# First output unit's loads, products and low parts inside the last MLP block, and rows of y in the order of need

## Chip, cores and metric

One core of one Trainium2 chip. The metric is the device time of one launch in microseconds, as the median of three runs; less is better. The kernel before takes 872.04 us (869.55 to 872.58).

## What is computed

One sequence of 2048 tokens of width 640, all in 32-bit floats:

```python
xn = layernorm(x)                               # no weights, eps 1e-5
q, k, v = split(xn @ wqkv)                      # 32 heads of 20
p = softmax(mask(q @ k.T * 20 ** -0.5))         # causal, window of 256 keys
s = heads_joined(p @ v) @ wo
h = relu(xn @ w1 + b1) ** 2                     # 640 -> 1536
g = silu(h @ w2 + b2)                           # 1536 -> 640
out = x + s * g
```

## The kernel before

Every product of the projections and of the MLP is made of three TensorE products: each operand is held as a rounded high part and the rest, its low part, and high times high, high times low and low times high are added up in PSUM.

A first phase normalizes and turns x, makes v, and makes q and k of the first heads. Then a loop of 256 steps (and a few more until its pipeline is empty) goes through 16 pairs of heads with 16 steps each: scores, row maxima, exponentials (`p32`) and, every fourth step, the product with v (`values`, written as `ops`). Its results go to DRAM as `o_d[g]`, one tensor for each quarter g of the tokens; row 20 of each head holds the sums of the exponentials.

Between these steps a generator, `filler`, hands out the other TensorE work one product at a time: the rest of q and k, then the MLP. The MLP's 1536 hidden columns are cut in two halves `hf`, the tokens in four blocks `b`; the eight blocks (hf, b) run one after the other, and the last one is (1, 1), tokens of tiles 4 to 7 (a tile is 128 tokens). A block makes its hidden part (`hps`), then eight groups of second products (`yps`): four tiles times two halves `nh` of the 640 columns. A group is evacuated by VectorE (line 969), which adds what the first half of the hidden columns gave (`yin`). `y` of the last block's four tiles stays in SBUF; `y` of the other twelve is stored to DRAM and read back later by `fetch_y`.

After the last block comes the output stage, `out_filler`. It has eight units u; unit u covers the two tiles `4*(u//2) + u%2` and that plus 2, so unit 0 is tiles 0 and 2, unit 1 is tiles 1 and 3. For a unit

- `load(u)` reads `o` with four transfers into `ob` and the inverse sums with one transfer, a broadcast over four rows of partitions, into `sums` (lines 1069 to 1080). The inverse sums of quarter g come from `invert`: a load of the sums, a reciprocal on VectorE, a store to `rec_d[g]`.
- `turn_out(u, 0)` multiplies `ob` by `sums` on VectorE in two cuts and rounds each to the high part `oT` on ScalarE (lines 1094, 1095). `turn_out(u, 1)` makes the low part on VectorE (1098) and, in the output stage, calls `silu(u)`: two activations on ScalarE over two tiles of y (1108).
- four groups (two tiles, two halves) of 15 products with `wo` follow on TensorE (`wops`, line 599). Each is evacuated by a product with y on VectorE (1157), then GpSimd adds x (1162) and the tile is stored.

`yps` and `wops` share three PSUM banks, so a group's first product waits for the evacuation of the group three before it. `wo` itself comes in five pieces (`raw`, three buffers), each rounded on ScalarE (773) and subtracted on VectorE (774); the fifth is `wo4h`, `wo4l`. All transfers go out from SP's queue, in the program's order; an SP instruction that must wait holds up all that follow. Every engine works its instructions in the order in which the Python code runs.

In `filler`, `late()` is called ahead of each of the last block's eight `yps` groups. Before the change it loads unit 0 as soon as quarter 0's inverse sums are on their way and returns, since all eight groups are handed out while the 256 steps still run; the lines behind its `return` never run. So `out_filler` begins with the remaining six reads of y, four reads of x, `silu(0)`, and then `turn_out(0, ...)`.

Of the kernel before, what the change touches and what calls it, by code (L numbers as in the profile page):

```python
# [15 lines left out]
P = 128  # L16
# [41 lines left out]
def attn_mlp_kernel(ctx: ExitStack, tc, x, wqkv, wo, w1, b1, w2, b2, out):  # L58
# [500 lines left out]
    def post(dst, src):  # L559
        posts.append((dst, src))  # L560
# [266 lines left out]
    def filler():  # L827
# [48 lines left out]
        xb, its = [xT[p][NB - 1] for p in range(2)], []  # L876

        def late():
            load(0)
            if state[2] < 10 ** 6:  # L880
                return
            j = lates[0]
            lates[0] += 1
            start_pieces()
            for f in release(1, True):
                f()
                held[0] -= 1
            invert(j)
            for _ in range(2):
                fetch_y()  # L890
            if j >= 2:
                load(1)
            if j == 3 or j == 5:
                load_res()
            if j >= 4:
                turn_out(0, 0)
            if j >= 5:
                turn_out(0, 1)

        for n, (hf, b) in enumerate(blocks):  # L900
            if n % NB == 0:
# [53 lines left out]
            for tt in range(4):  # L955
                t = b * 4 + tt
                place = [None]
                jobs = []

                def start(nh, hf=hf, t=t, place=place, idx=4 * (n - NB) + tt, end=n == NB - 1 and tt == 3, n=n, tt=tt):  # L960
                    sl = slice(nh * HALF, (nh + 1) * HALF)
                    ps = Acc(HALF, "yps")

                    def evac():
                        vload[0] += 0.5
                        if not nh:
                            place[0] = room_of("p32", "ysb") if n == last else wgt.tile([P, D], F32, tag="wgqh", name="ysb")
                        ysb = place[0]
                        nc.vector.tensor_add(ysb[:, sl], ps.tile, (yins[t] if hf else b2t)[:, sl])  # L969
                        ps.free(1.2)  # L970
                        if nh:
                            if n == last:
                                ybt[t] = ysb
                            else:
                                post(y_d[hf][:, t, :], ysb)
                            if hf:
                                del yins[t]
                                load_yin(idx + 2)
                            if end:
                                shut.discard("21")  # L980
                    return [ps, open_job(evac), 0]

                def product(jb, nh, fc):
                    ps, job, _ = jb
                    while (tt // 2, fc // 2) not in made:
                        if state[2] < 10 ** 6:
                            yield None
                        elif tasks:
                            finish()
                        else:  # L990
                            drain(backlog, 1)
                    for hp, wp in ((0, 0), (0, 1), (1, 0)):
                        jb[2] += 1
# [29 lines left out]

    lates = [0]

    def invert(j=99):
        for g in range(NB):
            over = state[2] >= 10 ** 6
            if not over and state[2] < stored(g) + 3:
                return  # L1030
            if g not in recs:
                rows = o_d[g].rearrange("p (h r) n -> (p h) r n", h=2)
                recs[g] = at2.tile([P, P], F32, tag="rec", name="rec")
                for par in range(2):
                    nc.sync.dma_start(recs[g][64 * par:64 * (par + 1)], rows[:, 32 * par + DH].rearrange("h (j n) -> h j n", n=P))
            elif recs[g] is not None and (state[2] >= stored(g) + 5 if not over else j >= 2 + g % 2):
                nc.vector.reciprocal(recs[g], recs[g])
                nc.sync.dma_start(rec_d[g].rearrange("a h (j n) -> (a h j) n", n=P), recs[g])
                recs[g] = None
# [4 lines left out]
        return wgt.tile([P, D], F32, tag=tag, name=name)  # L1044

    ybt = {}
    y_early = [((8 + j) % NT, w, i, j % 3) for j, (i, w) in enumerate([(i, w) for i in range(2) for w in "qk" for _ in range(3)])]
    y_room = []

    def fetch_y():  # L1050
        if y_early:
            t, w, i, k = y_early.pop(0)
            if not k:
                y_room.append((at, at1)[i].tile([P, S], F32, tag=f"{w}s{i}", name=f"y{w}{i}"))
            slot = y_room[-1][:, k * D:(k + 1) * D]
            nc.sync.dma_start(slot, y_d[1][:, t, :])
            ybt[t] = slot
# [4 lines left out]
    def load_res():  # L1062
        k = len(xts)
        if k < NT:
            t = in_order[k]
            xts[t] = room_of("p32" if k % 3 else "wgkh", "xres")
            nc.sync.dma_start(xts[t], x[t * P:(t + 1) * P, :])

    def load(u):
        if u in ld or u >= 2 * NB or recs.get(u // 2, 0) is not None:  # L1070
            return
        if u % 2 == 0:
            obs[u // 2] = bigp.tile([P, KC * BT], F32, tag="big", name=f"ob_{u // 2}")
        ob = obs[u // 2][:, u % 2 * 2 * D:(u % 2 + 1) * 2 * D].rearrange("p (c n) -> p c n", c=KC)
        sums = at2.tile([P, 2, P], F32, tag="osb" if u % 2 else "sums", name="sums").rearrange("p a n -> p (a n)")
        rows = o_d[u // 2].rearrange("p (h r) n -> (p h) r n", h=2)[:, 32 * (u % 2):32 * (u % 2) + VW]
        for k in range(4):
            nc.sync.dma_start(ob[32 * k:32 * k + H], rows[:, k:DH:4])  # L1078
        nc.sync.dma_start(sums, rec_d[u // 2][u % 2].unsqueeze(0).to_broadcast([4, H, MT]))
        ld[u] = (ob, sums)  # L1080
# [38 lines left out]
        return wo_part  # L1119

    def out_filler(wo_part):
        while y_early:
            fetch_y()
        while len(xts) < 4:
            load_res()
        silu(0)
        for u in range(2 * NB):
# [9 lines left out]
            for t2 in range(2):  # L1137
# [3 lines left out]
                for nh in range(2):  # L1141
# [8 lines left out]
                            mms.append((oT[u][:, op, c, t2 * P:(t2 + 1) * P], wo_part(wp, c)[:, sl]))  # L1150
                    yield from mm_group(ps, mms, 0.133)
                    invert()
                    for v in range(u + 1, u + 4):
                        load(v)

                    def evac(ps=ps, sl=sl, nh=nh, res=res, xt=xts[t], t=t):
                        nc.vector.tensor_mul(res[:, sl], ps, ybt[t][:, sl])
# [26 lines left out]
    with tc.manual_schedule(engines={E_.PE, E_.Activation, E_.DVE, E_.Pool, E_.SP}):  # L1184
# [7 lines left out]
        for s in range(steps):  # L1192
# [74 lines left out]
```

## Time and profile before

| | |
|---|---|
| median of three runs | 872.04 us |
| the profiled execution: its own time | 872.63 us |
| its span, first to last instruction | 870.8 us |
| TensorE busy in the span | 852.4 us (98%) |
| VectorE, ScalarE, GpSimd busy | 456.1, 423.1, 323.5 us |
| mean granted TensorE clock | 0.990 |

The profiled execution is 1.8 us longer than its span. Times inside it are microseconds from the span's start. A row of the timeline has start, duration, engine, line, operation, output<-inputs, count, and in brackets the engine's idle time before it and what ended it. A row of waits has the total, the times and the longest. "PEclk" is the granted clock, 1.00 is full speed. In a row of the table by stretches of time come: the stretch, its length, then the busy time of TensorE, of its weight loads, of VectorE, ScalarE and GpSimd, the clock, the DMA share and GB/s. Names of tiles have no numbers in the profile.

### The profile page before, as it was taken

What the parts mean: (1) busy time and instruction counts of PE and PEld (TensorE: products, weight loads), DVE (VectorE), ACT (ScalarE), POOL (GpSimd) and SP (SyncE); (2) the same over time, 40 slices, a digit from 0 to 9 for tenths busy, and PEclk for the clock granted to TensorE, in tenths of its full rate; (3) what the DMA queues carried; (4) which work ended last, traced back from release to release, by engine and by line L of the source; (5) the groups of instructions that cost most, each with busy time, mean ns of one, the idle gap of its engine ahead of it and who ended that gap; (6) DMA issues with size and microseconds to landing.
All of it is one profiled execution on the core that took longest, in us unless ns stands there. A gap on an engine that the chain in (4) does not pass through costs nothing.

```text
span 870.8 us, 26507 instructions
## 1 busy us (share of the span) xinstructions
PE 852.4 (98%) x10640; PEld 796.1 (91%) x10640; DVE 456.1 (52%) x1348; ACT 423.1 (49%) x808; POOL 323.5 (37%) x652
## 2 busy tenths in 40 slices
PE   9999999999999999999999999999999999997998
PEld 8999999888888999999999989999999999886997
DVE  7652136656567555455454466554454454334664
ACT  5222114545557754745735755835735646622321
POOL 6010002333333543533534533634634534502443
PEclk9999999999999999999999999999999999997999
DMA  7997587787799463273374255474475364458982
GB/s 266 307 400 281 167 224 245 267 256 258 242 276 303 100 213 120 61 233 91 102 226 153 78 160 150 143 233 128 112 243 132 113 205 136 127 161 207 228 225 77
DMA packets 94371, 166.50 MB, mean 191 GB/s; under 512 B 10920, under 2 KB 43816, under 8 KB 93224
## 3 DMA queue, kind: packets, MB, share of 16 engines
q1 hardware_dynamic: 94248, 164.80, 62.0%
q8 instruction: 84, 1.38, 0.7%
q14 instruction: 39, 0.32, 0.1%
HBM read 93.66 MB, written 70.52 MB: 189 GB/s over the span
## 4 chain that ended last, share of the span: by engine, by line
PE 93%; DMA 2%; DVE 2%; ACT 1%; issue 1%; SPq 1%; DVEq 0%
PE yps L468 20%; PE hps L468 20%; PE qkps L468 14%; PE ops L546 10%; PE vps L228 8%; PE wops L599 7%; PE stps L518 5%; PE sps L478 4%; PE qkps L205 3%; DMA ob<-o 1%; PE tps L172 1%; DMA yk<-y 1%; SPq L1078 0%; DVE junk L486 0%; DMA xt<-in_A_x_dram 0%
## 5 line engine op out<-in xcount | busy, mean ns | idle before, releaser
L486 DVE CUSTOM_DVE_ANT_0 junk<-sps,mask 128x384 bf16<-128x384 f32 (+2 forms) x512 | 272.6, 532 | 249.0 <-PE hps L468 71.9
L524 ACT ACTIVATE p<-stps 128x768 f32<-128x768 f32 (+2 forms) x256 | 197.3, 771 | 263.5 <-PE stps L518 212.1
L468 PE MATMUL yps<-w,hh 64*128 64x320 f32 x1536 | 230.8, 311 | 3.6 <-DVE ysb L969 3.2
L525 POOL TENSOR_SCALAR_AFFINE_SELECT p<-p 128x256 f32<-128x256 f32 x256 | 104.3, 407 | 335.3 <-ACT p L524 320.8
L468 PE MATMUL hps<-xb,w 64*128 64x256 f32 x2520 | 220.6, 283 | 0.0
L468 PEld LDWEIGHTS hps<-xb,w 64*128 64x128 f32 x2520 | 208.8, 187 | 5.5 <-issue 5.4
L468 PEld LDWEIGHTS yps<-w,hh 64*128 64x128 f32 x1536 | 186.5, 186 | 8.3 <-DVE ysb L969 4.7
L468 PE MATMUL yps<-w,hl 64*128 64x320 f32 x768 | 178.6, 311 | 0.0
L478 PE MATMUL sps<-ks,qs 60*128 60x384 f32 (+2 forms) x512 | 142.1, 341 | 0.3
L518 PE MATMUL stps<-qs,ks 62*128 62x384 f32 (+2 forms) x512 | 134.9, 332 | 0.0
L468 PEld LDWEIGHTS yps<-w,hl 64*128 64x128 f32 x768 | 117.2, 186 | 2.4 <-issue 2.3
L468 PE MATMUL qkps<-xT,wgkh 64*128 64x512 f32 x320 | 100.4, 395 | 0.0
L468 PE MATMUL qkps<-xT,wgqh 64*128 64x512 f32 x320 | 98.8, 393 | 0.0
L546 PE MATMUL ops<-p,vp 128*21 128x128 f32 (+1 forms) x2112 | 92.8, 313 | 0.0
L527 POOL TENSOR_SCALAR_AFFINE_SELECT p<-p 128x256 f32<-128x256 f32 x224 | 91.5, 409 | 0.0
L478 PEld LDWEIGHTS sps<-ks,qs 60*128 60x128 f32 x512 | 87.2, 185 | 2.8 <-DVE mt L486 1.3
L518 PEld LDWEIGHTS stps<-qs,ks 62*128 62x128 f32 x512 | 88.0, 188 | 0.5
L546 PEld LDWEIGHTS ops<-p,vp 128*21 128x21 f32 x2112 | 65.2, 100 | 22.1 <-issue 8.9
L599 PE MATMUL wops<-wo,oT 128*128 128x320 f32 x384 | 66.7, 326 | 8.4 <-ACT oT L1095 3.8
L228 PE MATMUL vps<-wv,xT 128*128 128x320 f32 x480 | 71.5, 308 | 0.0
L599 PEld LDWEIGHTS wops<-wo,oT 128*128 128x128 f32 x384 | 62.1, 202 | 9.4 <-ACT oT L1095 8.0
L228 PEld LDWEIGHTS vps<-wv,xT 128*128 128x128 f32 x480 | 70.5, 188 | 0.1
(104 smaller groups left out, 1174.2 us busy)
## 6 DMA issues: line engine op xcount, KB each, us to landing
ks<-k_d SPq DMA_DIRECT2D x64, 240.0 KB
qs<-q_d SPq DMA_DIRECT2D x64, 240.0 KB
xb<-xs SPq DMA_DIRECT2D x60, 256.0 KB
xs<-xT SPq DMA_DIRECT2D x8, 1280.0 KB
k_d<-shm SPq DMA_DIRECT2D x19, 512.0 KB
q_d<-shm SPq DMA_DIRECT2D x19, 512.0 KB
y<-ysb SPq DMA_DIRECT2D x28, 320.0 KB
o<-osb SPq DMA_DIRECT2D x64, 128.0 KB
```

What stands on the lines that cost most here:

```text
L172: nc.tensor.transpose(ps[:, t * P:(t + 1) * P], xns[t][:, c * P:(c + 1) * P], ident)
L205: nc.tensor.matmul(ps, wt[:, c, :], xT[part][b][:, c * BT + t0:c * BT + t0 + n], start=m == 1, stop=m == 3 * KC)
L228: nc.tensor.matmul(ps, xT[xp][b][:, c * BT + t * P: c * BT + (t + 1) * P], wv[wp][:, c, nh * HALF:(nh + 1) * HALF], start=first and m == 0 ...
L468: return nc.tensor.matmul(out, a[r], b_[r], skip_group_check=True, **kw)
L478: nc.tensor.matmul(ss[hh][:, :nk], qs[i][o, q * P:(q + 1) * P], ks[i][o, k0 * P:k0 * P + nk], start=True, stop=True)
L486: nc.vector.tensor_tensor_reduce(out=junk[:, :nk], in0=ss[hh][:, :nk], in1=mask[:, 3 * P - nk:], scale=1.0, scalar=-3.0e38, op0=ALU.add, o ...
L518: nc.tensor.matmul(tps[:, hh, :n], ks[i][o, kb * P:(kb + 1) * P], qs[i][o, kb * P:kb * P + n], start=True, stop=True)
L524: nc.scalar.activation(p32[:, :, :n], tps[:, :, :n], AF.Exp, scale=SCALE)
L525: nc.gpsimd.affine_select(p32[:, :, 0:P], p32[:, :, 0:P], pattern=[[0, 2], [1, P]], compare_op=ALU.is_ge, fill=0.0, base=0, channel_multip ...
L527: nc.gpsimd.affine_select(p32[:, :, 2 * P:], p32[:, :, 2 * P:], pattern=[[0, 2], [-1, P]], compare_op=ALU.is_gt, fill=0.0, base=0, channel ...
L546: nc.tensor.matmul(ot[r0:r0 + VW, c0:c0 + len(part), :], vps[p][:, kb // 4, kb % 4, hh, :], pt[:, hh, :].rearrange("p (t n) -> p t n", n=P ...
L599: nc.tensor.matmul(ps, a, b_, start=j == 0, stop=j == n - 1)
```

## The change

`late()` now counts its eight calls, j = 0 to 7: `load(0)` from j = 3, `load(1)` from j = 4, `turn_out(0, 0)` at j = 5, `turn_out(0, 1)` and `load(2)` from j = 6. The twelve early rows of y come in another order, the first six being tiles 0, 2, 1, 3, 8, 10, all read within the steps; the other six follow one by one, after each group of the output stage. `out_filler` no longer starts with reads of y, and loads at most one unit after each group. The `sums` tiles get three tags of their own in place of sharing the `osb` buffers; the first tile of x takes a `p32` buffer in place of `wgkh`.

```diff
         def late():
-            load(0)
-            if state[2] < 10 ** 6:
-                return
             j = lates[0]
             lates[0] += 1
-            start_pieces()
-            for f in release(1, True):
-                f()
-                held[0] -= 1
-            invert(j)
-            for _ in range(2):
-                fetch_y()
-            if j >= 2:
+            if j >= 3:
+                load(0)
+            if j >= 4:
                 load(1)
-            if j == 3 or j == 5:
-                load_res()
-            if j >= 4:
+            if j >= 5:
                 turn_out(0, 0)
-            if j >= 5:
+            if j >= 6:
                 turn_out(0, 1)
+                load(2)
...
                                 post(y_d[hf][:, t, :], ysb)
+                                if hf:
+                                    stored_y.add(t)
...
-    y_early = [((8 + j) % NT, w, i, j % 3) for j, (i, w) in enumerate([(i, w) for i in range(2) for w in "qk" for _ in range(3)])]
-    y_room = []
+    y_early = [((0, 2, 1, 3, 8, 10, 9, 11, 12, 14, 13, 15)[j], w, i, j % 3) for j, (i, w) in enumerate([(i, w) for i in range(2) for w in "qk" for _ in range(3)])]
+    y_room, stored_y = [], set()
 
     def fetch_y():
-        if y_early:
+        if y_early and y_early[0][0] in stored_y and (y_early[0][2] == 0 or whole[0]):
...
-            xts[t] = room_of("p32" if k % 3 else "wgkh", "xres")
+            xts[t] = room_of("p32" if k % 3 or k == 0 else "wgkh", "xres")
...
-        sums = at2.tile([P, 2, P], F32, tag="osb" if u % 2 else "sums", name="sums").rearrange("p a n -> p (a n)")
+        sums = at2.tile([P, MT if u // 2 % 3 == 0 else BT], F32, tag=("sums", "relu", "sq")[u // 2 % 3], name="sums")[:, :MT]
...
     def out_filler(wo_part):
-        while y_early:
-            fetch_y()
         while len(xts) < 4:
             load_res()
...
                     invert()
+                    fetch_y()
                     for v in range(u + 1, u + 4):
-                        load(v)
+                        if v not in ld:
+                            load(v)
+                            break
...
-            if s >= NP * NT - NT + LAG + 2 and len(ybt) < 6:
+            if s >= NP * NT - NT + LAG + 2:
                 fetch_y()
```

On TensorE no instruction moves: the order of all products is the same. On VectorE, at the last block's fourth evacuation (second half of tile 5; `yps_14347` in both programs), the order before is

```order
L969 TENSOR_TENSOR ysb_14447<-yps_14275,yin_13531 128x320
L774 TENSOR_TENSOR wo4l_14483<-raw_14333,wo4h_14482 128x640
L969 TENSOR_TENSOR ysb_14447<-yps_14347,yin_13531 128x320
L969 TENSOR_TENSOR ysb_14541<-yps_14397,yin_14372 128x320
L969 TENSOR_TENSOR ysb_14541<-yps_14473,yin_14372 128x320
L969 TENSOR_TENSOR ysb_14644<-yps_14521,yin_14498 128x320
L969 TENSOR_TENSOR ysb_14644<-yps_14561,yin_14498 128x320
L1094 TENSOR_TENSOR ob_0_14268<-ob_0_14268,sums_14269 128x512
L1094 TENSOR_TENSOR ob_0_14268<-ob_0_14268,sums_14269 128x768
L1098 TENSOR_TENSOR oT_0_14665<-ob_0_14268,oT_0_14665 128x512
L1098 TENSOR_TENSOR oT_0_14665<-ob_0_14268,oT_0_14665 128x768
```

and now, at the same place,

```order
L960 TENSOR_TENSOR ysb_14453<-yps_14268,yin_13531 128x320
L1087 TENSOR_TENSOR ob_0_14340<-ob_0_14340,sums_14341 128x512
L1087 TENSOR_TENSOR ob_0_14340<-ob_0_14340,sums_14341 128x768
L774 TENSOR_TENSOR wo4l_14494<-raw_14326,wo4h_14493 128x640
L960 TENSOR_TENSOR ysb_14453<-yps_14347,yin_13531 128x320
L1091 TENSOR_TENSOR oT_0_14479<-ob_0_14340,oT_0_14479 128x512
L1091 TENSOR_TENSOR oT_0_14479<-ob_0_14340,oT_0_14479 128x768
L960 TENSOR_TENSOR ysb_14561<-yps_14403,yin_14372 128x320
L960 TENSOR_TENSOR ysb_14561<-yps_14484,yin_14372 128x320
L960 TENSOR_TENSOR ysb_14664<-yps_14541,yin_14509 128x320
L960 TENSOR_TENSOR ysb_14664<-yps_14581,yin_14509 128x320
```

Unit 0's two products now stand ahead of the fourth evacuation, its two low parts right behind it. (Lines of the new program are 6 to 9 lower than those of the old one there.) On ScalarE, around the last piece of `wo`, the order before is

```order
L524 ACTIVATE p32_14467<-stps_14463 128x2x128
L773 ACTIVATE wo4h_14482<-raw_14333 128x640
L551 ACTIVATE osb_14578<-ops_1358 128x256
L1108 ACT_TABLE_LOAD
L1108 ACTIVATE yq1_14647<-yq1_14647 128x640
L1108 ACTIVATE yk1_14651<-yk1_14651 128x640
L1095 ACTIVATE oT_0_14665<-ob_0_14268 128x512
L1095 ACTIVATE oT_0_14665<-ob_0_14268 128x768
```

and now

```order
L524 ACTIVATE p32_14473<-stps_14469 128x2x128
L1088 ACTIVATE oT_0_14479<-ob_0_14340 128x512
L1088 ACTIVATE oT_0_14479<-ob_0_14340 128x768
L773 ACTIVATE wo4h_14493<-raw_14326 128x640
L551 ACTIVATE osb_14598<-ops_1358 128x256
L1101 ACT_TABLE_LOAD
L1101 ACTIVATE yq0_13794<-yq0_13794 128x640 x2
L1088 ACTIVATE oT_1_14680<-ob_0_14340 128x512
```

The rounding of unit 0 has moved ahead of the piece `wo4h`, and the two activations of y read a tile (`yq0`) that is filled within the steps. On SP's queue, from the store of quarter 0's inverse sums on, the order before is

```order
L1038 DMA rec_1359<-rec 128x128
L564 DMA o_86<-osb 128x256
L1078 DMA ob_14268<-o_85 32x5x256 x4
L1079 DMA sums<-rec_1359 128x1x256
L749 DMA raw<-in_A_wo_dram 32x640 x4
L1035 DMA rec<-o_86 64x1x128 x2
L749 DMA raw<-in_A_wo_dram 32x640 x4
L875 DMA yin<-y_83 128x640
L1038 DMA rec_1360<-rec 128x128
```

and now

```order
L1031 DMA rec_1359<-rec 128x128
L564 DMA o_86<-osb 128x256
L749 DMA raw<-in_A_wo_dram 32x640 x4
L1028 DMA rec<-o_86 64x1x128 x2
L749 DMA raw<-in_A_wo_dram 32x640 x4
L1071 DMA ob_14340<-o_85 32x5x256 x4
L1072 DMA sums<-rec_1359 128x1x256
L875 DMA yin<-y_83 128x640
L1071 DMA ob_14340<-o_85 32x5x256 x4
L1072 DMA sums<-rec_1359 128x1x256
```

Unit 0's five transfers now stand behind both pieces of `wo`, and unit 1's five follow behind one read of `yin`; before, unit 1's stood behind the reads of y and x of the output stage.

More of the change, by code (lines that the diff above doesn't have):

```diff
@@ L1024, in attn_mlp_kernel, with invert @@
     lates = [0]
-    def invert(j=99):
+    def invert():
         for g in range(NB):
@@ L1035, in invert @@
                     nc.sync.dma_start(recs[g][64 * par:64 * (par + 1)], rows[:, 32 * par + DH].rearrange("h (j n) -> h j n", n=P))
-            elif recs[g] is not None and (state[2] >= stored(g) + 5 if not over else j >= 2 + g % 2):
+            elif recs[g] is not None and (state[2] >= stored(g) + 5 if not over else True):
                 nc.vector.reciprocal(recs[g], recs[g])
```

## Prediction

> **What bounds the kernel now.** The page's head says that TensorE is busy for 98% of the span, so there is nothing to win except where it stops. I read its waits first, from the last MLP block on (stopped for, times, longest, in us):
>
> ```profile
> PE wops L599 <- ACT oT L1095: 3.8, 1, 3.8
> PE wops L599 <- DVE res L1157: 3.7, 1, 3.7
> PE yps L468 <- DVE ysb L969: 1.7, 1, 1.7
> PE wops L599 <- DVE oT L1098: 0.9, 1, 0.9
> ```
>
> Three of the four belong to the output stage's first two units. The timeline places them:
>
> ```profile
> 781.27 0.31 PE L468 MATMUL yps<-w,hl 64*128 64x320 f32 x1
> 781.61 0.49 DVE L969 TENSOR_TENSOR ysb<-yps,yin 128x320 f32<-128x320 f32 x1 [2.09 <-PE yps L468]
> 784.03 0.74 ACT L1108 ACTIVATE yk<-yk 128x640 f32<-128x640 f32 x1 [2.40 <-DMA yk<-y]
> 784.67 1.35 ACT L1095 ACTIVATE oT<-ob 128x512 fp32r<-128x512 f32 x2
> 785.34 3.76 PE L599 MATMUL wops<-wo,oT 128*128 128x320 f32 x12 [3.77 <-ACT oT L1095]
> 785.32 1.69 DVE L1098 TENSOR_TENSOR oT<-ob,oT 128x512 fp32r<-128x512 f32 x2 [1.75 <-ACT oT L1095]
> 786.93 0.95 DVE L1037 RECIPROCAL rec<-rec 128x128 f32<-128x128 f32 x1
> 797.97 1.56 DVE L1094 TENSOR_TENSOR ob<-ob,sums 128x512 f32<-128x512 f32 x2 [7.54 <-DMA ob<-o]
> 800.88 0.53 PE L599 MATMUL wops<-wo,oT 128*128 128x320 f32 x2 [3.73 <-DVE res L1157]
> 809.19 1.92 PE L599 MATMUL wops<-wo,oT 128*128 128x320 f32 x12
> 864.19 1.92 PE L599 MATMUL wops<-wo,oT 128*128 128x320 f32 x12
> 866.24 0.31 PE L599 MATMUL wops<-wo4h,oT 128*128 128x320 f32 x1
> ```
>
> The first stop runs from 781.58 to 785.34: ScalarE waits for a row of y, and the rounding of unit 0 stands behind that activation. The second runs from 797.15 to 800.88: VectorE waits for unit 1's `ob`, and the evacuations that free a bank stand behind it. The clock makes both dearer. In this table (stretch, length, busy times, then PEclk, DMA share, GB/s) I cut at the changes of the granted clock:
>
> ```profile
> 757.10:760.52 3.42, 1.68 (x24) 1.38 (x22) 2.88 (x3) 1.45 (x3) 2.02 (x3) 1.00 0.78 174
> 760.52:763.93 3.41, 3.41 (x27) 3.21 (x23) 0.49 (x1) 1.35 (x2) 0.41 (x2) 0.50 0.56 136
> 784.41:791.24 6.83, 5.90 (x21) 5.68 (x22) 3.00 (x4) 1.61 (x3) 0.73 (x1) 0.50 0.55 201
> 794.66:798.07 3.41, 2.49 (x17) 2.23 (x16) 0.10 (x1) 0.00 (x0) 0.00 (x0) 1.00 1.13 183
> 801.48:808.31 6.83, 6.02 (x23) 6.02 (x23) 6.52 (x8) 2.91 (x5) 4.27 (x4) 0.50 0.96 243
> ```
>
> Each change lies on a grid of 3.41 us. A cell in which TensorE was idle for 1.74 of 3.42 us is followed by one at half clock; one with 0.92 idle is not. After each of the two long stops the half clock lasts two cells.
>
> Undisturbed, 25 groups take 864.19 - 809.19 = 55.0 us, so 2.20 us each. Six groups stand between 781.58 and 809.19: 27.6 us, where 13.2 would do. The start of the output stage **loses 14.4 us**, stops and half clock together. Behind 809.19 it runs without a stop.
>
> **The change, part by part.**
>
> *y in the order of need.* Unit 0's activations read `yq0`, which is filled within the steps, and unit 0's high and low parts are due before the last evacuation. So the first stop goes, and what is late next is the last evacuation itself: the first `wops` group takes the bank of the last `yps` group. From the rows at 781.27 and 781.61, TensorE then stops from 781.58 to 782.10 and a little: **0.55 us** stay. That is less idle time than the 0.92 that kept the clock.
>
> *Unit 1 loaded early.* Its transfers leave SP within the MLP, not at 795, so VectorE can multiply them right after the last evacuation. From there 1.55 for the products, 0.95 for a reciprocal, 0.5 for the first evacuation and 1.7 for the low parts (rows above) make 4.7 us, and unit 0's four groups take 8.8: 4 us to spare. Unit 2, loaded early too, is due 8.8 us after that. The second stop goes. The displaced reads of y (six times 320 KB by the answer on DMA issues) go out one for each group; against them stand two units of `ob` and `sums` (two times 4 x 160 + 128 KB) that left the stage, so it has 0.4 MB more to move. I cost them at nothing: they hide behind unit 0's and 1's products, and the first of them is wanted in unit 5. If that cover failed, the wait would be a DMA's at a unit's start (a rival, below).
>
> *The x buffer, the tags of `sums`, one load for each group.* Nothing: their instructions stay off TensorE's path, under the 2.20 us groups.
>
> *What is added: unit 0 ahead of an evacuation.* This is the new wait. VectorE's two products for unit 0 now stand ahead of `wo4l` and of the fourth evacuation; `wo4l` needs `wo4h`, which stands behind both roundings on ScalarE. The seventh `yps` group takes the fourth's bank, so TensorE waits for all this. The order before had little to spare there:
>
> ```profile
> 768.02 0.22 PE L518 MATMUL stps<-qs,ks 62*128 62x128 f32 x1
> 773.79 1.28 PE L546 MATMUL ops<-p,vp 128*21 128x256 f32 x28
> 766.95 0.49 DVE L969 TENSOR_TENSOR ysb<-yps,yin 128x320 f32<-128x320 f32 x1 [1.13 <-issue]
> 768.62 0.73 ACT L773 ACTIVATE wo4h<-raw 128x640 fp32r<-128x640 f32 x1
> 769.38 0.83 DVE L774 TENSOR_TENSOR wo4l<-raw,wo4h 128x640 fp32r<-128x640 f32 x1 [1.94 <-ACT wo4h L773]
> 770.12 0.48 DVE L969 TENSOR_TENSOR ysb<-yps,yin 128x320 f32<-128x320 f32 x1
> ```
>
> Between the `stps` and the `ops` rows stand 77 half products at an even pace (768.1 to 773.75), and the seventh group's first is the 41st: it starts at 771.0. The fourth evacuation ended at 770.6. Now, if unit 0's data are there at T, VectorE is through with its products at T + 1.55, ScalarE's second rounding at T + 2.25 (half of 1.35 each), `wo4h` at T + 2.95, `wo4l` at T + 3.75, the evacuation at T + 4.25. T comes from SP's queue:
>
> ```profile
> 753.80 1.89 SPq L1078 DMA_DIRECT2D ob<-o x4
> 755.73 0.58 SPq L1079 DMA_DIRECT2D sums<-rec  x1
> 756.35 1.86 SPq L749 DMA_DIRECT2D raw<-in_A_wo_dram  x4
> 758.25 1.17 SPq L1035 DMA_DIRECT2D rec<-o  x2
> 760.93 1.25 SPq L749 DMA_DIRECT2D raw<-in_A_wo_dram  x3
> SPq L749 <- DMA sums<-rec: 0.9, 1, 0.9
> 754.78 0.82 DVE L774 TENSOR_TENSOR wo<-raw,wo 128x640 fp32r<-128x640 f32 x1 [3.26 <-ACT wo L773]
> 757.14 1.58 DVE L774 TENSOR_TENSOR wo<-raw,wo 128x640 fp32r<-128x640 f32 x1 [1.54 <-ACT wo L773]
> ```
>
> The two pieces of `wo` go first now. The first waits for its buffer until 755.6 (`wo` at 754.78) and takes 1.86 to issue, to 757.5; the two `rec` loads end at 758.7; the second piece waits until 758.72 (`wo` at 757.14) and ends at 760.6. There `ob` begins, 6.8 us later than before. Before, SP stood still until 760.9 because `sums` had not landed: 7.1 us after `ob`'s first issue. That makes 767.7; a piece of `wo` is still on the way ahead of it, so I take T = 768.0. The evacuation ends at 772.3 and the seventh group stops for **1.3 us**.
>
> The bounds of T are wide, since landing was seen once. These steps of the chain of waits show transfers from issue to landing (start, us):
>
> ```profile
> 754.27 3.04 DMA ob<-o
> 777.83 6.18 DMA yk<-y
> 793.97 4.01 DMA ob<-o
> ```
>
> `sums` is issued by 763.1. With 3.0 us it is there before VectorE is free (766.95 + 0.49), T = 767.4, and the stop is 0.7. With the slowest, 6.2, T = 769.2 and the stop is 2.5. I keep 1.3, nearest to the row of `sums` itself.
>
> The Trainium skill, "DMA: Bandwidth & Descriptors", section "Rules for kernel authors", says that a transfer whose outermost dimension is a broadcast of c copies uses at most c of the 16 engines; `sums` has such a dimension of 4, and its late landing before agrees. It speaks against putting `sums` ahead of an evacuation. An estimate from that page's 27 GiB/s for each engine is 1.1 us for its 128 KB where 16 engines would take 0.3; the sum would be the same, as T is taken from SP's wait.
>
> *Behind the stop.* The eighth group follows 2.65 us later and needs the fifth evacuation, which stands behind the two low parts: 1.69 + 0.49 = 2.2 us. It is in time. All that is later moves by the 1.3.
>
> **The sum.** -14.4 + 0.55 + 1.3 = -12.5 us. Against the profiled execution's 872.63 that is **860.1 us**; its span would be 858.3, the 1.8 us around it the same. The median of the runs, 872.04, lies 0.6 lower than that execution, within its runs' own spread of 3 us; I leave the forecast at 860.1.
>
> **Rivals.**
>
> *No new stop.* If T + 4.25 fits under 771.0, the time is 858.8. It speaks against it that VectorE is busy until 767.44, which alone leaves 0.7.
>
> *The new stop costs clock.* 1.3 us idle lie between the 0.92 that kept the clock and the 1.74 that lost it. A cell at half clock does 1.7 us less work: 861.8. It needs the stop to lie in one cell of the grid, for which its length leaves about 6 in 10, and a limit under 1.3. The Trainium skill, "TensorE: Matmul & The Clock Gate", section "HAM oscillation", gives as the abstract rule that only idle gaps over some 3.4 us lose the clock. By it this rival could not be, and the time would stay 860.1. The trace disagrees: the 1.74 us at 757 were enough.
>
> *The second stop stays in part.* If DMA is the limit of the output stage (share 0.96 to 1.13 above, and 0.4 MB more), a unit's `ob` or a reciprocal's load comes late and VectorE holds evacuations again. The second stop cost 809.19 - 797.15 - 4.4 = 7.6 us; half of it is 863.9, all of it 867.7.
>
> *Nothing comes of it.* If the first stop were set by something that neither y nor unit 0 explains, the two would go on: 872 and, with the new stop, 873.
>
> *Slower: the in-order wait at `sums`.* VectorE's first product waits for `sums`, and every later evacuation behind it. Each microsecond by which T is later than 768.0 is one more of TensorE's stop, and half of one more while the clock is down. It eats the whole gain from T = 780 on (768.0 + 12.5), or from about 776 with the clock; at T = 784 the time is at least 876. The slowest transfer of the rows above would have to be three times slower.
>
> **How the numbers follow.** Forecast 860.1: 0.50. No new stop, 858.8: 0.14. Half clock, 861.8: 0.22. Part of the second stop, 863.9 to 867.7: 0.09. Nothing: 0.03. Slower: 0.02. Where the clock's grid lies differs from run to run; the stop at 757 costs 1.7 us or nothing by it, so the low end is 858.8 - 1.7 = 857.1. The high end takes in a stop of 2.5 with the half clock (863.0) and half of the second stop: 864.5. Left out are the dearer half of that rival and the last two, about 0.10, and what is misjudged besides. A measurement of this kernel can tell about 0.5%, 4.4 us, from no change: faster is all below 867.7, which is 0.93; within it 0.05; slower 0.02.
>
> **What would show it.** In the profile after: `wops` starts about 0.6 us behind the last `yps`, and its 32 groups run at 2.20 us with no wait for `oT` or for a row of y; the clock stays at 1.00 from 783 on; a stop of TensorE near 771, ended by the evacuation `ysb`, with VectorE's products waiting for a DMA until 768. A `wops` wait for `oT` in unit 1, a DMA share of 1 with ScalarE waiting for y, or a stop at 771 of over 3 us would prove me wrong, each at the step named.

## The result and the profile after

The changed kernel takes **861.85 us** (median of four runs, 860.56 to 863.13) against 872.12 of the kernel before beside it: ratio 0.989, interval 0.986 to 0.991. The forecast was 860.1, its range 857.1 to 864.5. The profiled execution took 860.56, its span 858.8; the forecast was made against the profiled execution of before, 872.63, so the change took 12.07 where 12.5 stood in the sum. Between the two medians it is 10.3; the profiled execution is the fastest of its four.

TensorE's waits from 740 on, in the kernel after (total, times, longest):

```profile
PE yps L468 <- DVE ysb L960: 4.8, 2, 3.0
PE wops L599 <- DVE ysb L960: 0.7, 1, 0.7
PE yps L468 <- ACT relu L925: 0.2, 1, 0.2
```

No group of the output stage waits for `oT` or behind `res` any more. What is left is one handover of 0.7, and two waits for an evacuation inside the last block. The timeline of TensorE places them:

```profile
758.98 0.56 PE L468 MATMUL yps<-w,hh 64*128 64x320 f32 x3 [1.74 <-DVE ysb L960]
...
772.49 0.41 PE L468 MATMUL yps<-w,hh 64*128 64x320 f32 x1 [3.01 <-DVE ysb L960]
...
783.92 2.00 PE L599 MATMUL wops<-wo,oT 128*128 128x320 f32 x12 [0.67 <-DVE ysb L960]
```

The first is the old stop at 757. The second, 3.01 us, is the new one, ahead of the seventh `yps` group. VectorE's timeline shows what it stands for:

```profile
768.11 1.56 DVE L1087 TENSOR_TENSOR ob<-ob,sums 128x512 f32<-128x512 f32 x2 [2.40 <-DMA sums<-rec]
771.21 0.83 DVE L774 TENSOR_TENSOR wo4l<-raw,wo4h 128x640 fp32r<-128x640 f32 x1 [1.53 <-ACT wo4h L773]
771.95 0.48 DVE L960 TENSOR_TENSOR ysb<-yps,yin 128x320 f32<-128x320 f32 x1
```

Unit 0's products wait for `sums` until 768.11 (forecast 768.0), and the fourth evacuation, behind them and `wo4l`, ends at 772.43 (forecast 772.3). The last piece of the chain that ended last is the whole output stage in one:

```profile
783.92 70.65 PE wops L599 x480
```

32 groups in 70.65 us are 2.21 each. And by stretches (length, busy times of TensorE, its loads, VectorE, ScalarE, GpSimd, then PEclk, DMA share, GB/s), the two around the stops, and one of the output stage:

```profile
757.16:760.58 3.42, 1.68 (x24) 1.60 (x24) 2.79 (x4) 1.41 (x2) 1.76 (x3) 1.00 0.44 125
760.58:763.99 3.41, 3.41 (x59) 2.81 (x59) 1.37 (x3) 1.44 (x2) 0.77 (x2) 1.00 0.88 218
...
767.40:770.82 3.42, 2.08 (x28) 1.81 (x24) 1.56 (x2) 1.75 (x3) 0.05 (x1) 1.00 0.88 186
770.82:774.23 3.41, 1.74 (x24) 1.74 (x26) 3.02 (x5) 0.35 (x1) 0.00 (x0) 1.00 0.38 89
...
794.71:798.12 3.41, 3.41 (x26) 3.41 (x25) 3.41 (x4) 2.19 (x4) 1.38 (x2) 1.00 1.01 353
```

The clock stays at 1.00 behind both stops, though TensorE was idle for 1.74 of the 3.42 us at 757, as in the kernel before, where half clock followed. In the stretch of the output stage the DMA share is 1.01, and TensorE does not stop.

### The profile page after: what moved, and what is told of

Same layout as the page of the kernel before. It is cut to its first block, busy times and chain, and to the rows that moved or that the text cites. A ratio compares the mean times of both kernels' runs of the same rounds, so it can differ in the third digit from the quotient of the medians.

```text
span 858.8 us, 26512 instructions
## 1 busy us (share of the span) xinstructions
PE 845.2 (98%) x10640; PEld 790.8 (92%) x10640; DVE 455.7 (53%) x1348; ACT 423.2 (49%) x808; POOL 323.0 (38%) x652
## 5 line engine op out<-in xcount | busy, mean ns | idle before, releaser
L930 POOL TENSOR_TENSOR hl<-sq,hh 128x512 fp32r<-128x512 f32 x48 | 62.3, 1298 | 21.2 <-ACT sq L929 21.2
L599 PE MATMUL wops<-wo,oT 128*128 128x320 f32 x384 | 61.6, 309 | 0.7 <-DVE ysb L960 0.7
```

Source lines behind the costliest of these rows:

```text
L599: nc.tensor.matmul(ps, a, b_, start=j == 0, stop=j == n - 1)
L930: nc.gpsimd.tensor_sub(hh[1][:, :BT], sq, f32(hh[0]))
```

## Experiments

All kernels are edits of the changed one. "Last block" is the time in the profiled execution from the `yps` row that waits 0.2 us for `relu` (753.97 in the kernel after) to the first `wops`; "output stage" goes from there to the end of the span. These two do not hold what varies ahead of the block: that first row lies anywhere from 753.9 to 755.6 in these executions. e1 to e4, e5 to e8 and e9 to e12 each shared a chip, and their own runs of before (medians 871.12, 871.25 and 870.29), to which the ratios are.

| kernel | median, us (runs) | ratio to before | interval | last block | output stage |
|---|---|---|---|---|---|
| before | 872.12 | 1 | | 31.16 | 85.46 |
| after | 861.85 (4) | 0.989 | 0.986 to 0.991 | 29.95 | 74.88 |
| e1 products one call later | 858.62 (4) | 0.986 | 0.984 to 0.987 | 26.54 | 75.93 |
| e2 unit 0 loaded first | 859.77 (4) | 0.987 | 0.985 to 0.988 | 27.64 | 74.88 |
| e3 `sums` in four | 861.17 (4) | 0.988 | 0.987 to 0.990 | 29.15 | 74.98 |
| e4 old order of y, burst | 866.67 (6) | 0.994 | 0.992 to 0.995 | 31.22 | 76.25 |
| e5 after, again | 862.46 (4) | 0.990 | 0.989 to 0.992 | 32.13 | 74.88 |
| e6 unit 0 loaded later | 869.84 (11) | 0.998 | 0.997 to 1.000 | 39.32 | 74.86 |
| e7 e1, reciprocals later | 858.98 (4) | 0.986 | 0.984 to 0.988 | 28.10 | 74.87 |
| e8 new order of y, burst | 865.69 (6) | 0.993 | 0.991 to 0.995 | 29.77 | 80.87 |
| e9 no products in the block | 861.78 (6) | 0.989 | 0.988 to 0.991 | 29.25 | 76.99 |
| e10 no early loads | 873.89 (12) | 1.004 | 1.002 to 1.005 | 27.70 | 91.22 |
| e11 e7, low parts of `wo` later | 857.47 (5) | 0.985 | 0.982 to 0.987 | 25.24 | 74.94 |
| e12 after, low parts of `wo` later | 863.56 (6) | 0.991 | 0.990 to 0.993 | 31.97 | 74.88 |

My theory of the new stop was the in-order one: an evacuation stands behind products that wait for a DMA. The rivals: the data are late wherever the products stand; the products themselves, not their wait, hold the evacuation.

**e1: the products one call later.**

```diff
-            if j >= 5:
-                turn_out(0, 0)
             if j >= 6:
-                turn_out(0, 1)
+                turn_out(0, 0)
                 load(2)
+            if j >= 7:
+                turn_out(0, 1)
```

> The changed kernel with unit 0's products and roundings (and its low parts) issued one call of the last block later, so that on VectorE the fourth evacuation and the subtraction for wo4l stand ahead of the products that wait for sums; nothing else differs. In-order theory (the 3.0 us stop of TensorE before the seventh yps group is the products' wait for sums at 768.1, with the fourth evacuation queued behind it): the fourth evacuation ends at about 770.6 as in the kernel before, the stop near 769.5 to 772.5 goes, and the time falls by about 3 us, from the profiled 860.56 to about 857.5, in the medians from 861.9 to about 859. Rival (the data are late wherever the products stand): the products now stand ahead of the fifth evacuation, so the stop only moves to the eighth yps group, and the time stays within 1 us of the changed kernel's.

TensorE's waits of more than 0.2 us from 740 on:

```profile
PE yps L468 <- DVE ysb L960: 1.7, 1, 1.7
PE wops L599 <- DVE res L1151: 0.8, 1, 0.8
PE wops L599 <- DVE ysb L960: 0.7, 1, 0.7
```

and VectorE's timeline:

```profile
768.34 0.48 DVE L960 TENSOR_TENSOR ysb<-yps,yin 128x320 f32<-128x320 f32 x1
768.74 1.55 DVE L1087 TENSOR_TENSOR ob<-ob,sums 128x512 f32<-128x512 f32 x2
...
788.87 0.95 DVE L1030 RECIPROCAL rec<-rec 128x128 f32<-128x128 f32 x1 [3.91 <-DMA rec<-o]
```

The stop is gone and did not move to the eighth group: the evacuation now runs at 768.34, and the products find `sums` there when VectorE gets to them. The last block is 3.41 us shorter. The profiled execution took 858.17, not 857.5: a reciprocal waits 3.91 us for `rec`, three evacuations stand behind it, and TensorE stops for 0.8 at 789.5. Part of the gain was lost to the same kind of stop one stage later.

**e2: unit 0's load first.**

```diff
-            if j >= 3:
-                load(0)
+            load(0)
```

> The changed kernel with unit 0's loads (ob and sums) left where the kernel before has them, ahead of the two pieces of wo on SP; the products stay ahead of the fourth evacuation as in the changed kernel. If the stop before the seventh yps group is set by when sums lands (768.1), and that by SP's order, then the products run at about 765.7, right behind the third evacuation, the fourth evacuation ends near 770.0, and the stop shrinks from 3.0 us to about 0.5: about 858 against 860.56. Rival (what holds the fourth evacuation is the work itself that now stands ahead of it, products, roundings and wo4h, and not the wait): the stop stays at 2 us or more and the time within 1 us of 860.56.

VectorE and TensorE:

```profile
766.73 1.55 DVE L1086 TENSOR_TENSOR ob<-ob,sums 128x512 f32<-128x512 f32 x2
...
770.74 0.48 DVE L959 TENSOR_TENSOR ysb<-yps,yin 128x320 f32<-128x320 f32 x1
```

```profile
771.28 0.41 PE L468 MATMUL yps<-w,hh 64*128 64x320 f32 x1 [0.69 <-DVE ysb L959]
```

With the data there, the products run right behind the third evacuation, and the stop is 0.69 with the products, the rounding and `wo4l` all still ahead. So the work alone costs 0.7 and the wait cost the other 2.3. The time of 858 was not reached (859.36 in the profile): the last block is shorter by 2.31, but it began 1.1 us later.

**e3: `sums` in four plain transfers.**

```diff
-        nc.sync.dma_start(sums, rec_d[u // 2][u % 2].unsqueeze(0).to_broadcast([4, H, MT]))
+        for k in range(4):
+            nc.sync.dma_start(sums[32 * k:32 * k + H], rec_d[u // 2][u % 2])
```

> The changed kernel with the broadcast load of sums (one transfer with an outer dimension of 4) written as four plain transfers of 32 rows, for every unit; the bytes are the same and SP issues three instructions more for a unit, about 1.2 us. If the broadcast transfer is slow because few engines carry it, sums lands 1 to 1.5 us earlier (about 766.7 in place of 768.1), the stop before the seventh yps group is about 1.6 us and the time about 859.2. Rival (sums lands late because SP issues it last, behind four transfers of ob, and the load of unit 0 as a whole sets the time): products start at 768.1 or later by up to 1.2 us, the stop is 3.0 to 4.2 us, and the time is 860.5 to 862.

SP's issue of `sums` in the kernel after, and in this one:

```profile
762.34 0.58 SPq L1072 DMA_DIRECT2D sums<-rec  x1
```

```profile
763.03 1.82 SPq L1073 DMA_DIRECT2D sums<-rec  x4
```

and VectorE in this one:

```profile
767.44 0.49 DVE L960 TENSOR_TENSOR ysb<-yps,yin 128x320 f32<-128x320 f32 x1 [0.69 <-PE yps L468]
767.85 1.55 DVE L1088 TENSOR_TENSOR ob<-ob,sums 128x512 f32<-128x512 f32 x2
```

The products did not wait: the four transfers, issued by 764.85, had landed by 767.85, within 3.0 us. In the kernel after, the one broadcast, issued by 762.92, kept the products until 768.11, 5.2 us. But this execution had half clock behind 757, so the third evacuation came only at 767.44, and the stop, 0.69, does not compare with 3.01. It compares with that of e5 below, which had the same half clock: there the stop is 2.11, and the products start 5.6 us behind the end of the broadcast's issue (in e8, e11 and e12 5.0 to 5.7). The median, 861.17, lies 0.7 and 1.3 below the changed kernel's two, inside the spread of their runs. On the landing the broadcast theory holds, with one execution of four transfers against five of the broadcast; on the time the run is inconclusive.

**e4 and e8: the rows of y in one burst.** Both have the loop; e4 has the old order too.

```diff
-    y_early = [((0, 2, 1, 3, 8, 10, 9, 11, 12, 14, 13, 15)[j], w, i, j % 3) for j, (i, w) in ...]
+    y_early = [((8 + j) % NT, w, i, j % 3) for j, (i, w) in ...]
...
     def out_filler(wo_part):
+        while y_early:
+            fetch_y()
```

> The changed kernel with the old order of the rows of y (from row 8 on) and the old loop that issues all that is left of them at the start of the output stage; unit 0's loads, products and low parts stay early. Theory A (unit 0's oT are made within the MLP, so no rounding is queued on ScalarE behind an activation that waits for y; y alone is worth nothing here): wops starts within 1 us of the last evacuation, and the time is within 1 us of the changed kernel's 860.56. Theory B (as the prediction's first term put it, y in the order of need is what removes the first stop): ScalarE waits for yq0 at the start of the output stage until 784 or later, and TensorE stops there again for 2 to 4 us, with half clock behind it: 863 to 868.

> The changed kernel with its new order of the rows of y, but with all that are left of them issued at once at the start of the output stage, as the kernel before does: between the old-order run (866.7 median) and the changed kernel (861 to 862) this says which half of that edit cost the 5 us. If it is the burst (six rows of y and five of x in one piece on SP and on the DMA engines, ahead of the last rec load, whose reciprocal then holds the evacuations): 864 to 867 and a wops stop behind res near 795. If it is the order (ScalarE waits for the rows yq of the first units, and unit 1's rounding stands behind): 860.5 to 862.

e4 lost 4.8 us to the first median of the changed kernel, e8 3.2 to the second, on its own chip. In e4 neither theory held whole. ScalarE does wait for a row of y at the start of the output stage, as in the kernel before:

```profile
785.77 0.74 ACT L1101 ACTIVATE yq<-yq 128x640 f32<-128x640 f32 x1 [5.27 <-DMA yq<-y]
```

But unit 0's `oT` is made by then, and `wops` starts 0.68 behind the last `yps`: no first stop came back. And yet y is worth something. TensorE's wait in the output stage:

```profile
PE wops L599 <- DVE res L1153: 1.1, 1, 1.1
```

e8 shows the same at a larger size (its runs go from 863.80 to 868.15, and the profiled one, 867.97, is the second longest), in the waits, in SP's timeline, in VectorE's and in the chain that ended last:

```profile
PE wops L599 <- DVE res L1153: 4.2, 1, 4.2
```

```profile
781.22 1.34 SPq L1049 DMA_DIRECT2D yq<-y  x3
782.60 1.38 SPq L1049 DMA_DIRECT2D yk<-y  x3
785.52 2.75 SPq L1060 DMA_DIRECT2D xres<-in_A_x_dram  x5
...
789.55 1.43 SPq L1028 DMA_DIRECT2D rec<-o  x2
```

```profile
797.15 0.95 DVE L1030 RECIPROCAL rec<-rec 128x128 f32<-128x128 f32 x1 [7.33 <-DMA rec<-o]
```

```profile
790.46 6.60 DMA rec<-o
```

Eleven reads leave SP ahead of the last `rec`. It lands at 797.06, VectorE stands at its reciprocal for 7.33 us, and the evacuations that free a bank stand behind. Counted from the first `wops`, this `rec` leaves SP at 4.22 and its reciprocal starts at 11.82; in the kernel after it is 2.65 and 5.49. So 1.6 of the 6.3 us are SP's queue, and the rest lies between issue and landing, with a DMA share of 1.02 from 786 to 791 where the kernel after has 0.48. The burst costs, and the order of the rows, once unit 0's products are early, shows no effect: e4 and e8 have the same ratio within their intervals.

**e5: the changed kernel again.**

> The changed kernel again, unedited, to stand beside the three below on the same chip: median between 860.5 and 862.5, with the 3.0 us stop before the seventh yps group in it when the stop at 757 kept the clock, and about 1.3 us of it when that one lost it.

This execution, 862.74, is the other form of the same program. Stretches, then VectorE and TensorE:

```profile
756.36:759.77 3.41, 1.67 (x22) 1.37 (x22) 2.81 (x3) 2.00 (x3) 2.58 (x4) 1.00 0.42 120
759.77:763.19 3.42, 3.42 (x30) 3.42 (x28) 0.57 (x2) 0.32 (x1) 0.00 (x0) 0.50 0.79 204
...
770.01:773.43 3.42, 1.31 (x18) 1.05 (x16) 1.88 (x4) 1.47 (x2) 0.00 (x0) 1.00 0.43 111
773.43:776.84 3.41, 3.41 (x28) 3.41 (x28) 1.63 (x3) 0.00 (x0) 0.00 (x0) 0.50 0.45 123
```

```profile
768.57 1.77 DVE L1087 TENSOR_TENSOR ob<-ob,sums 128x512 f32<-128x512 f32 x2 [1.29 <-DMA sums<-rec]
```

```profile
773.15 0.42 PE L468 MATMUL yps<-w,hh 64*128 64x320 f32 x1 [2.11 <-DVE ysb L960]
```

Here the stop at 757 does cost half clock. TensorE comes to the seventh group 1.6 us later (773.15 - 2.11 = 771.04, against 769.48), as the prediction had it, and stops for 2.11; that stop lies in one cell of the grid and costs another cell at half clock. The stop is longer than the 1.3 I expected, by `sums` (768.57) and by the products, 1.77 for 1.56.

**e6: unit 0's load two calls later**, a dose of the wait.

```diff
-            if j >= 3:
+            if j >= 5:
                 load(0)
-            if j >= 4:
                 load(1)
-            if j >= 5:
                 turn_out(0, 0)
```

> The changed kernel with unit 0's load issued two calls later, together with unit 1's: on SP it now stands behind a row of yin, the write of a reciprocal and an attention store; nothing else moves on any engine. This is a dose of the wait at sums. In-order theory: ob's first transfer leaves SP at about 765.7 (the attention store's osb is ready at 765.3) in place of 760.5, so sums lands about 5.2 us later, at 773.3; the fourth evacuation is held as much longer, TensorE's stop grows from 3.0 to about 8 us and costs one or two cells at half clock besides: 860.6 + 5.2 + 1.7 to 3.4 = 867.5 to 869.2. Rival (sums lands at 768 for a reason that is not SP's order, such as the DMA's own backlog): the stop grows by less than 1 us and the time stays under 862.

```profile
776.03 1.56 DVE L1085 TENSOR_TENSOR ob<-ob,sums 128x512 f32<-128x512 f32 x2 [8.25 <-DMA ob<-o]
```

```profile
780.40 0.63 PE L468 MATMUL yps<-w,hh 64*128 64x320 f32 x1 [8.85 <-DVE ysb L958]
```

The products start at 776.03, 7.46 later than in e5 (I had put 5.2; the attention store ahead of `ob` left SP at 767.4, not 765.7), and the execution took 870.46, 7.72 more. Nearly the whole gain is eaten at T = 776, the point that the prediction's slower rival named. The rival's mechanism is real; only T was not that late.

**e7: e1, and each reciprocal of the output stage two calls behind its load.**

```diff
...
+            elif recs[g] is not None and over and aged.setdefault(g, 0) < 2:
+                aged[g] += 1
             elif recs[g] is not None and (state[2] >= stored(g) + 5 if not over else True):
```

> As the run with the products one call later, and in the output stage each reciprocal is issued two calls behind its load rather than one, so that the second and third evacuations of wops stand ahead of the reciprocal that waited 3.9 us for rec. In-order theory: the 0.8 us stop of TensorE at 789.5 in that run (wops waits for res, queued behind the reciprocal) goes, and the time falls from its 858.2 to about 857.3, the median from 858.6 to about 857.8. Rival (rec is needed soon by a later unit, so that its delay is paid there): another wait of 0.8 us or more shows behind 790, and the time is 858.2 or more.

The 0.8 us stop is gone and none took its place: the output stage is 74.87 again. The profiled execution took 858.76, with half clock behind 757 (last block 28.10); the fastest run was 857.48. By the medians e1 and e7 are the same; the 857.8 that I expected of e7 was not reached.

**e9: no products in the block,**

```diff
-            if j >= 5:
-                turn_out(0, 0)
             if j >= 6:
-                turn_out(0, 1)
                 load(2)
```

**and e10: no early loads either**, while y keeps the new order and goes one row a group.

```diff
         def late():
-            j = lates[0]
-            lates[0] += 1
-            if j >= 3:
-                load(0)
-            if j >= 4:
-                load(1)
-            if j >= 5:
-                turn_out(0, 0)
-            if j >= 6:
-                turn_out(0, 1)
-                load(2)
+            load(0)
```

> The changed kernel with units 0, 1 and 2 loaded early as in it, but with unit 0's products, roundings and low parts left at the start of the output stage, behind the last evacuation; no other engine's order moves. If early products pay nothing here, since they cost a stop of TensorE before the seventh yps group of about what they save: no stop at 769, but wops starts only when the first product (0.7), its rounding (0.65) and its low part (0.7) are through, about 1.9 us later than the 0.7 of the changed kernel; about 860 when the clock is kept, median 860 to 861.5, no worse than the changed kernel. If early products are worth their place, it is 1.5 us or more above the changed kernel.

> The changed kernel with unit 0 loaded where the kernel before loads it and nothing else of the early calls: units 1 and 2 are loaded in the output stage, unit 0's products stand behind the last evacuation; the new order of y, one row for each group, stays. If y alone carries the gain: within 1 us of the run without products in the block. If the early load of unit 1 carries its own part, as the prediction's second stop says: VectorE waits in unit 0 for ob of unit 1 with evacuations behind it, TensorE stops for 3 to 4 us near 791 with half clock behind that, and the median is 864 to 868.

TensorE at the start of e9's output stage:

```profile
783.51 0.56 PE L599 MATMUL wops<-wo,oT 128*128 128x320 f32 x2 [1.84 <-ACT oT L1085]
784.32 2.85 PE L599 MATMUL wops<-wo,oT 128*128 128x320 f32 x10 [0.25 <-DVE oT L1088]
```

1.84 and 0.25, with half clock behind them, and no stop at 769: 861.78, the changed kernel's own time and 0.3 over what I had put. Where the change puts them, the early products are worth what they cost; one call later (e1) they are worth about 3 us. e10 I missed by 6 us: I expected 864 to 868, and it is slower than the kernel before. Its waits, and three steps of its chain:

```profile
PE wops L599 <- DVE res L1141: 8.1, 4, 4.2
```

```profile
788.71 5.14 DMA sums<-rec
800.14 8.47 DMA xres<-in_A_x_dram
808.63 9.87 DMA yk<-y
```

Not one stop but four, behind transfers that take 5 to 10 us: the chain goes on to 829 through `sums`, a row of x and a row of y. So the early loads of units 1 and 2 carry the gain: against e9 they are worth 12.1 us. What the new order of y is worth alone e10 does not show, since it is not the kernel before with that order: it also keeps one load and one row of y after each group. How far it is the queue on SP and how far the DMA engines' own load was not tried apart.

**e11 and e12: the low parts of `wo` later**, on e7 and on the changed kernel alone.

```diff
     def piece_pair(tag, hi, lo, src):
         def go(raw):
             nc.scalar.activation(hi(), raw, AF.Copy)
-            nc.vector.tensor_sub(lo(), raw, f32(hi()))
+            if tag == "o":
+                later(0.5, lambda: nc.vector.tensor_sub(lo(), raw, f32(hi())))
+            else:
+                nc.vector.tensor_sub(lo(), raw, f32(hi()))
```

> As the run with products and reciprocals later, and the subtraction that makes a low part of wo is issued half a microsecond of matmul cost later than its rounding, so that on VectorE the first evacuation of the last block stands ahead of the subtraction that it waited for at 757. TensorE's 1.74 us stop at 757, which is in every kernel so far, goes, and with it the half clock that follows in some executions. Where nothing else is late: 1.7 us under 857.5 (that run's fastest), so 855.8, and every run near that, with a median of about 856. Rival (the subtraction's delay hands its lateness on to the next buffer of raw, the second piece of wo and the loads behind it on SP): a new stop, and 857 or more.

> The unedited changed kernel with only that delay of wo's low parts: products stay ahead of the fourth evacuation. If the time at which TensorE passes the seventh yps group is set by SP's queue and sums (768.1) and not by TensorE, then what the stop at 757 no longer takes is given back there: the stop before the seventh group grows from 3.0 to about 4.7 us, and the time stays at 860.5 to 862. Rival (the two stops are independent): 1.7 us less, 858.8 or below in the fastest runs.

All that TensorE waits for in e11 from 740 on:

```profile
PE wops L599 <- DVE ysb L963: 0.7, 1, 0.7
PE yps L468 <- ACT relu L928: 0.2, 1, 0.2
```

The stop at 757 is gone; the last block takes 25.24, the shortest. The fastest run, 855.95, is where I had put it; the median, 857.47, is 1.5 higher than expected, and its interval overlaps e7's. Of all versions it is the fastest; its interval, 0.982 to 0.987, lies below that of e5 and meets that of the first runs of the changed kernel, 0.986 to 0.991, at the edge. In e12 the same edit gained nothing:

```profile
769.47 1.56 DVE L1090 TENSOR_TENSOR ob<-ob,sums 128x512 f32<-128x512 f32 x2 [4.75 <-DMA sums<-rec]
```

```profile
773.85 0.63 PE L468 MATMUL yps<-w,hh 64*128 64x320 f32 x1 [5.36 <-DVE ysb L963]
```

TensorE came to the seventh group earlier (13.64 us behind the block's first row, in the kernel after 15.51) and waited for the same event, 5.36 us in place of 1.74 and 3.01 (or 2.11); the stop ended no earlier (19.00 for 18.52). And the long stop cost two cells at half clock: the block takes 2.02 more than in the kernel after, and 1.54 of this lie behind the end of the stop. The median, 863.56, is not better than the changed kernel's but 1.1 to 1.7 above it (the ratios' intervals overlap), and over the 862 that I had allowed, since I had left that clock out.

## Why the prediction was right, and where not

**The first stop** went, as forecast; 0.67 is left for the 0.55 worked out. But the reason given first, y in the order of need, was not the one that counts. e9 has that order and still waits 1.84 and 0.25 for unit 0's `oT`. e4 has the old order and ScalarE's wait for y, but the products made within the block, and waits 0.68: these alone remove the stop, and they are paid for at the new one.

**The second stop** went, through the early load of units 1 and 2: without it (e10) four stops come. In the kernel after no group waits for `oT` or `res`. Of the 4 us to spare for unit 1, 3.7 were there: its low parts are done at 789.12, its first group starts at 792.80.

```profile
786.88 2.24 DVE L1091 TENSOR_TENSOR oT<-ob,oT 128x512 fp32r<-128x512 f32 x2
```

**The reads of y at nothing**: right for one row after each group, with a DMA share of 1.01 beside a TensorE that does not stop and a ScalarE that waits for no row of y. It was not free by itself. e8 loses 3.2 us to the changed kernel on the same chip when they leave SP together, through the last `rec` and not through ScalarE. I had the cover named as the products of units 0 and 1; what decides in e8 is a small load that is issued behind the reads. The x buffer and the tags of `sums` were not tried apart.

**The new stop**: the mechanism, in-order VectorE and `sums`, is shown by e1, e2, e6 and e12, and T was right within 0.1 (e5: 0.6). Mis-sized is one term, 1.3 us for a measured 3.01; the mark that the prediction set itself for this step, over 3 us, is just met. The step that failed is "the seventh group's first is the 41st: it starts at 771.0". That time was read from an execution of before with a cell at half clock behind 757. Without it TensorE is there at 769.48, and as the products' wait ends by SP's queue (768.11, in e5 768.57) and not by TensorE, most of what the clock gave was taken at the stop. In e5, with the half clock, the arrival is 771.04 and the stop 2.11.

So the sum for the profiled execution is -14.4 + 0.67 + 3.01, less the 1.7 of half clock that did not come: -12.4, for a measured -12.07. That it came so near 860.1 is in part luck: the stop is 1.7 longer than forecast, and the clock that was kept gave 1.7. The same sum for e5 is -14.4 + 0.67 + 2.11 + 1.7 = -9.9, or 862.7; it took 862.74.

**The rivals.** "The new stop costs clock", 861.8, is what e5's execution shows, with its half-clock cell, and both medians (861.85 and 862.46) lie nearer to it than to the 860.1 I held likeliest. Of the changed kernel's first four runs, the two with a mean granted clock of 1.000 took 860.56 and 861.55, those with 0.997 and 0.998 took 862.14 and 863.13. The low end of the range, 857.1, took 1.7 off for a kept clock at 757. e12 shows that this could not be had: the time won ahead of the products' wait for a DMA was lost in it.

## To carry to other kernels

Work that is moved forward into an in-order queue brings its waits along: ask when its last operand lands, and what stands behind it; one place further back (e1) kept the gain and saved 3 us. When a stop is set by a transfer, speeding up what comes before it gains nothing until the transfer or its place is moved (e12, then e11). Reads that are off the path still held up the small load that was issued behind them (e8), so spread them.

## What was not expected of the hardware

The clock's cells of 3.41 us go by TensorE's busy time in each, not by the length of a stop. Between 747 and 801 of these executions, a cell at full clock with 1.74 us busy (the kernel after) or more was always followed by full clock, one with 1.43 (e12) or less by half clock, and with 1.63 to 1.69 it went either way. The stop of 1.74 at 757 leaves 1.67 to 1.69 of its cell busy when it lies inside one. So it falls into the margin, and costs 1.7 us or nothing: with 1.67 the clock was kept in e2 and e8 and lost in e5 and e7. What decides inside the margin no run shows; it is not only where the grid lies, as the prediction had it. The 3.01 us of after lie across two cells, 2.08 and 1.74 busy, and cost no clock; the 2.11 of e5, in one cell with 1.31 busy, did. The Trainium skill, "TensorE: Matmul & The Clock Gate", section "HAM oscillation", gives gaps over some 3.4 us as what to avoid; by the rows above a gap of 2.11 is enough, and one of 3.01 can be free.

The Trainium skill, "DMA: Bandwidth & Descriptors", section "Rules for kernel authors", says that a leading broadcast of c copies keeps a transfer to at most c engines. e3 agrees by its time: 5.2 us from issue to use for the broadcast of 4, at most 3.0 for the same bytes in four plain transfers, at 1.2 us more of SP's time. How many engines carried either no run shows.
